# Transformer block with windowed attention and a spatially gated MLP: scores in 1024-column units with paired masks, overlapping contraction chunks, a new buffer plan and a new order

## The chip, the cores and the metric

The kernel runs on one core of one Trainium2 chip. The core has a matrix engine (TensorE, in the profile PE for multiplications and PEld for its weight loads), a vector engine (DVE), an activation engine (ACT), a general engine (POOL) and a queue that issues transfers (SP). TensorE writes to PSUM, eight banks of 512 float32 columns on 128 partitions; ACT and DVE read it from there. The metric is the device time of one execution, in microseconds (us), lower is better. The kernel before takes 363.6 us, the median of three runs (363.48 to 365.13).

## The reference

The input `x` has 2048 rows (tokens) of 448 columns, in bfloat16. A conditioning vector `c` gives six vectors of 448: shift and scale (`sa`, `ca`) and a gate `ga` for the first half, `sb`, `cb`, `gb` for the second.

```python
mod = (_silu(c) @ w_mod).reshape(c.shape[0], 6, 1, -1)
h = _layernorm(x) * (1 + ca) + sa
x = x + ga * _A_ref(h, A_wqkv, A_wo)          # 16 heads of 28; a row sees itself and the 255 rows before it
h = _layernorm(x) * (1 + cb) + sb
x = x + gb * _B_ref(h, ...)
# _B_ref: z = gelu(h @ w_in); z1 = z[:, :896]; z2 = layernorm(z[:, 896:])
#         g = w_sp @ z2 + b_sp;  result (z1 * g) @ w_out      (w_sp is 2048 x 2048)
```

## The kernel before, in words

The 2048 rows are 16 tiles of 128. All work is described as operations with dependencies, a priority and an assumed duration (class `Planner`, lines 55 to 211); when the kernel is built, a list scheduler places each operation on its engine at the earliest assumed start, ties and near ties by priority, and gives out PSUM banks and buffer slots as their last users end. The result is one fixed program for each engine, in which each instruction waits for semaphores. So an engine never goes past an instruction that waits, and the order on the chip is the order that the assumed durations led to. SP's queue is such a program too: a transfer's issue counts as 100 ns in the plan.

The work has four stages.

1. **Start.** Weights and `x` are loaded (lines 377 to 394), the conditioning vector is brought into columns by two transfers of single elements, `silu` is taken, and 32 one-column multiplications make shift and scale (`mod_cols`, 429). For each block of 512 rows (`NB` is 4) the rows are normalised (`ln1`, 498), transposed by TensorE (`transp`, 514), shifted and scaled on the way out of PSUM into `hT`, and multiplied by the weights (`qkv`, 548). The 448 rows of the contraction are cut into chunks of 128, 128, 128 and 64 (`KC`): four multiplications for each result. Q and K land in `QKT` with each head on its own 32 partitions, V in `Vaug` with a column of ones.
2. **Attention** (line 600 on), mixed with the projections of later blocks. For a tile j of queries and each of eight pairs of heads, one unit: up to 3 x 2 small multiplications (`S`, 611, on 32 rows of the array each) give the scores against key tiles j-2, j-1 and j; one ACT instruction takes the exponential of up to 768 columns (629); POOL zeroes what lies outside the window in tile j-2 and in tile j, with one instruction each (638, 640); six multiplications with 29 columns (`PV`, 652) add up the result and the sum of weights. After eight units, DVE divides (665, 667), SP issues a transposing transfer (671), four multiplications by `wo` follow (678), DVE adds to `x` (682), the second normalisation is taken (684 to 687), and a second transposing transfer writes `hT` anew (689). Scores have two pairs of banks (`B_S`), `PV` one bank, everything else three.
3. **MLP in** (line 742 on), after the last scores: `z2` for 16 tiles, `z1` for 28 blocks of 128 x 512, `gelu` on ACT, the normalisation of `z2` on DVE and POOL. Shift and scale of the second half were folded into `w_in` beforehand (702 to 714).
4. **Spatial product and MLP out** (line 782 on): 28 results of 16 multiplications each with the transposed `w_sp`, bias and product on DVE, 16 results of 7 multiplications by `w_out`, and the store. `w_sp` is loaded by 32 transposing transfers (728), which SP issues in the attention stage, two runs of 12 and one of 8.

## Time and profile before

One execution was profiled. Its span, from the first to the last instruction, is 362.0 us; the page gives no other time for that execution, and the runs' median is 1.6 us above the span.

| stretch of the span, us | what runs | length | TensorE busy | ACT busy | granted clock |
|---|---|---|---|---|---|
| 0 to 12.6 | loads, shift and scale | 12.6 | 2.45 | 1.58 | 1.00 |
| 12.6 to 62 | projections, first tiles | 49.4 | 46.76 | 27.65 | 0.97 |
| 62 to 92 | attention | 30.0 | 22.88 | 13.38 | 0.66 |
| 92 to 137 | attention and projections | 45.0 | 43.40 | 30.04 | 0.99 |
| 137 to 189.7 | attention alone | 52.7 | 42.90 | 36.46 | 0.50 |
| 189.7 to 240.1 | MLP in | 50.4 | 50.11 | 30.40 | 0.99 |
| 240.1 to 358.1 | spatial product, MLP out | 118.0 | 117.47 | 0.60 | 1.00 |
| 358.1 to 362 | last results and stores | 3.9 | 0.03 | 0.00 | 0.92 |

The granted clock is the share of full speed at which TensorE was allowed to run. A multiplication's duration contains its way through the array, so times are read here from one start to the next: where eight multiplications of 448 columns follow each other in the MLP stage the next group starts 1.52 us later, 0.190 us each. Where a line is L427, it is the helper `mm` through which all multiplications go; the tile names tell them apart.

### The profile page before, as it was taken

To read this page: it belongs to the slowest core of one execution; us is meant where nothing else is said; L and a number is where in the kernel's file an instruction comes from. 1 tells how busy PE (TensorE), PEld (TensorE's weight loads), DVE (VectorE), ACT (ScalarE), POOL (GpSimd) and SP (SyncE) were. 2 spreads that over 40 slices of the span, in tenths; PEclk is the share of its full clock that TensorE was granted. 3 is DMA by queue.
4 is the path that set the end of the run, shared out by engine and by line. 5 is a ranking of instruction groups with operands and counts; after the bars stand their busy time and mean duration, and the time that the engine had idled before them with its cause. 6 is when DMAs were issued, how large, how long until landed. Compare 5 with 4: busy or idle time off the path is not lost.

```text
span 362.0 us, 6545 instructions
## 1 busy us (share of the span) xinstructions
PE 326.0 (90%) x2620; PEld 156.6 (43%) x2648; DVE 171.7 (47%) x390; ACT 140.1 (39%) x197; POOL 117.4 (32%) x294
## 2 busy tenths in 40 slices
PE   0799998758999996698999999999999999999995
PEld 0424453423445553354444444444444444444442
DVE  1857645834576552232237887503324333233323
ACT  0346655633547675588784576640000000000000
POOL 5113344752648775588771212200000000000000
PEclk9999998955999995555559999999999999999999
DMA  6992399991212039813311000000001001001001
GB/s 200 344 347 82 59 177 168 185 173 29 45 31 30 16 40 167 118 31 46 30 31 29 16 0 2 2 0 0 2 0 51 2 0 53 0 0 39 14 0 51
DMA packets 60061, 23.62 MB, mean 65 GB/s; under 512 B 52224, under 2 KB 58560, under 8 KB 60032
## 3 DMA queue, kind: packets, MB, share of 16 engines
q1 hardware_dynamic: 59552, 23.21, 30.6%
q8 instruction: 21, 0.34, 0.4%
q10 hardware_dynamic: 480, 0.00, 0.1%
q14 instruction: 8, 0.07, 0.1%
HBM read 8.78 MB, written 1.84 MB: 29 GB/s over the span
## 4 chain that ended last, share of the span: by engine, by line
PE 80%; DMA 7%; SPq 4%; ACT 3%; DVE 3%; issue 2%; POOL 0%; DVEq 0%; ACTq 0%
PE ps L427 80%; DMA oT<-o_sb 5%; SPq L728 4%; ACT PT L629 3%; DMA cT_sb<-in_c_dram 2%; DVE w_out_sb L716 1%; DVE st_all L490 1%; DVE hT L534 0%; ACT L419 0%; DVE fin L820 0%; DVE WQK L542 0%; POOL rs_all L486 0%; DVE x_sb L682 0%; DVE sc_rep L421 0%; DVEq L829 0%
## 5 line engine op out<-in xcount | busy, mean ns | idle before, releaser
L629 ACT ACTIVATE PT<-ps 128x768 bf16<-128x768 f32 (+2 forms) x128 | 93.8, 770 | 55.3 <-PE ps L427 54.3
L427 PE MATMUL ps<-w_spA,z_73 128*128 128x512 bf16 x329 | 76.6, 379 | 0.4
L638 POOL TENSOR_SCALAR_AFFINE_SELECT PT<-PT 128x256 bf16<-128x256 bf16 x112 | 46.5, 415 | 52.9 <-ACT PT L629 51.9
L640 POOL TENSOR_SCALAR_AFFINE_SELECT PT<-PT 128x256 bf16<-128x256 bf16 x128 | 52.8, 414 | 21.3 <-ACT PT L629 21.2
L798 DVE TENSOR_TENSOR tmpg<-ps,bsp_bc 128x512 bf16<-128x512 f32 x28 | 19.4, 692 | 73.6 <-PE ps L427 73.6
L427 PE MATMUL ps<-QKT 32*128 32x128 bf16 x720 | 46.0, 257 | 6.2 <-ACT PT L629 4.8
L427 PEld LDWEIGHTS ps<-w_spA,z_73 128*128 128x128 bf16 x336 | 32.8, 98 | 39.6
L427 PE MATMUL ps<-hT,WQK 128*128 128x512 bf16 (+1 forms) x115 | 39.1, 412 | 1.5 <-ACT PT L629 0.4
L427 PE MATMUL ps<-Vaug,PT 128*128 128x29 bf16 x720 | 34.3, 183 | 2.3 <-POOL PT L640 1.9
L486 POOL TENSOR_TENSOR rs_all<-ve_all,neghalf 128x1 f32<-128x1 f32 (+1 forms) x39 | 23.0, 602 | 40.9 <-DVE ve_all L484 40.8
L427 PEld LDWEIGHTS ps<-Vaug,PT 128*128 128x128 bf16 x720 | 26.9, 101 | 20.4 <-POOL PT L640 7.6
L427 PE MATMUL ps<-wo_sb,oT 128*128 128x448 bf16 x64 | 23.2, 473 | 10.5 <-DMA oT<-o_sb 10.5
L427 PEld LDWEIGHTS ps<-QKT 32*128 32x128 bf16 x720 | 22.8, 105 | 22.0 <-PE ps L427 17.0
L682 DVE TENSOR_TENSOR x_sb<-ps,x_sb 128x448 bf16<-128x448 f32 x16 | 10.0, 624 | 40.3 <-PE ps L427 40.3
L427 PE MATMUL ps<-w_spB,z_73 128*128 128x512 bf16 x109 | 28.3, 379 | 0.2
L427 PE MATMUL ps<-w_in_sb,hT 128*128 128x448 bf16 (+1 forms) x128 | 26.8, 356 | 0.0
L427 PE MATMUL ps<-hT,w_in_sb 128*128 128x512 bf16 (+1 forms) x107 | 25.5, 379 | 0.3
L490 DVE BATCH_NORM_STATS2 st_all<-x_sb 128x6 f32<-128x448 bf16 x32 | 19.1, 611 | 6.6 <-DMA x_sb<-in_A_x_dram 6.3
L427 PE MATMUL ps<-w_out_sb,z1T 128*128 128x448 bf16 x112 | 21.8, 352 | 0.0
L567 DVE CAST QKT<-ps 128x512 bf16<-128x512 f32 x22 | 15.1, 688 | 13.3 <-PE ps L427 13.2
L490 DVE BATCH_NORM_STATS2 st_all<-z2raw 128x6 f32<-128x448 bf16 x32 | 18.7, 610 | 5.4 <-ACT z2raw L756 5.0
L776 ACT ACTIVATE z1T<-ps 128x512 bf16<-128x512 f32 x28 | 16.7, 597 | 8.6 <-PE ps L427 8.6
(65 smaller groups left out, 250.8 us busy)
## 6 DMA issues: line engine op xcount, KB each, us to landing
x_sb<-in_A_x_dram SPq DMA_DIRECT2D x4, 448.0 KB, 8.5
out_dram<-fin SPq DMA_DIRECT2D x16, 112.0 KB, 1.7
w_in_sb<-in_B_w_in_dram SPq DMA_DIRECT2D x1, 1344.0 KB, 11.4
wqkv_sb<-in_A_wqkv_dram SPq DMA_DIRECT2D x1, 1008.0 KB, 9.5
wmod_sb<-in_w_mod_dram SPq DMA_DIRECT2D x1, 1008.0 KB, 9.3
w_out_sb<-in_B_w_out_dram SPq DMA_DIRECT2D x1, 784.0 KB, 12.8
wmod_sb<-in_w_mod_dram SPq DMA_DIRECT2D x1, 672.0 KB, 7.3
bsp_bc<-in_B_b_sp_dram SPq DMA_DIRECT2D x1, 512.0 KB, 13.4
```

The costliest lines, as they stand in the source:

```text
L427: return e.matmul(out_, lhsT=lhsT, rhs=rhs, start=st, stop=sp, **kw)
L486: return P.op(name + "rs", prio, [("pool", 500 + 130 * (t1 - t0 - 1), lambda e: e.tensor_tensor(rs_all[:, slot, t0:t1], ve_all[:, slot, t0 ...
L490: st = [P.op("%sst%d" % (name, i), prio, [("dve", dve_ns(D, base=145), lambda e, i=i, s_=s_: e.bn_stats(st_all[:, slot, t, i, :], s_()))], ...
L567: return e.tensor_copy(QKT[:, g, tb * 512:(tb + 1) * 512], ps[:, ten.slot, :])
L629: return e.activation(ptv(pt)[:, :, 0:nb, :], ps[:, ten.slot:ten.slot + 2, 0:nb * 128].rearrange("p h (b q) -> p h b q", q=128), ACT.Exp, ...
L638: e.affine_select(out=v[:, :, 0, :], in_=v[:, :, 0, :], pattern=[[0, 2], [-1, 128]], compare_op=ALU.is_gt, fill=0.0, base=0, channel_multi ...
L640: return e.affine_select(out=v[:, :, nb - 1, :], in_=v[:, :, nb - 1, :], pattern=[[0, 2], [1, 128]], compare_op=ALU.is_ge, fill=0.0, base= ...
L682: x1_op[j] = P.op("x1_%d" % j, pr, [("dve", 624, lambda e, j=j, wt=wt: e.tensor_tensor(x_sb[:, j, :], ps[:, wt.slot, 0:D], x_sb[:, j, :], ...
L716: t_woutg = P.op("woutg", 4.3, [("dve", dve_ns(7 * D), lambda e: e.tensor_tensor(w_out_sb[:], w_out_sb[:], ps[:, ten_g2.slot, 0:D].unsquee ...
L728: return e.dma_start_transpose(out=dst[:, hf * 1024:(hf + 1) * 1024], in_=B_w_sp[hf * 1024:(hf + 1) * 1024, si * 128:(si + 1) * 128])
L776: z1_op[(ft, tb)] = P.op("z1g%d_%d" % (tb, ft), pr, [("act", act_ns(512), lambda e, tb=tb, ft=ft, ten=ten: e.activation(z1T[:, ft, tb * 51 ...
L798: a = P.op("ga%d_%d" % (tb, ft), pr, [("dve", 692, lambda e, tb=tb, ten=ten, tg=tg: e.tensor_tensor(tmpg[:, tg.slot, :], ps[:, ten.slot, : ...
```

## The change

Nearly every function is written anew. In the order of the stages:

- **Start.** The conditioning vector is loaded as one row and turned into columns by four small multiplications; the tables of `silu` and of the exponential are loaded ahead of their first use; 30 multiplications of zeros (`warm`) may fill TensorE's idle time. Loads that only the second half needs (`w_in`, the second part of `w_mod`, `w_out`, the bias) are issued after the first four transposing transfers. The blocks are 256, 256, 512, 512 and 512 rows. From the third block on, rows are normalised on POOL, transposed by a transfer on SP, and shifted and scaled in place by DVE or POOL (`modulate`).
- **Chunks.** The 448 rows of a contraction are held as four chunks of 128 that overlap (rows 0, 128, 192 and 320 on), so that two results (`Pair`) take three whole multiplications each, and their rests, 64 rows in the upper and 64 in the lower half of the array, one double step. The order takes the rests of two pairs together. Q, K, V, `z2` and `z1` are made so. Other contractions use four chunks of 112.
- **Attention.** A unit is one key tile with eight heads: 8 multiplications into two banks, one exponential of 1024 columns that reads the two banks element by element in turn, so that the results of two heads lie side by side. For key tiles j and j-2 POOL masks 512 such pairs as 32-bit words with one instruction; for j-1 none. The eight `PV` multiplications read their stationary operand with a step of two elements. There are 90 units in place of 128, 60 masks in place of 240.
- **Rest.** Shift and scale of the second half are no longer folded into `w_in` but applied to `hT`, two tiles at a time; `PV`, `wo` and the projections share banks 4 to 7. `w_sp` is fetched in 32 transfers of 512 x 256: 16 go into parts of `QKT` as their last scores are done (4 each after tiles 5, 9, 13 and 15), 16 into `Vaug` and `PT` after the last `PV`. Assumed durations and priorities are new (SP's transposing issue now counts 1250 to 1340 ns). Stage 4 has the same multiplications.

```diff
+WINDOW = {'pe': 60.0, 'act': 0, 'dve': 200.0, 'pool': 0, 'sp': 100}
+PARAMS = {
+    'ln1': (-43.888, -27.425, 1.986, 3.811, 5.635),
+    'tr': (-50.231, -2.58, 0.847, 3.1, 3.297),
+    'pj': (-38, -0.204, 1.282, 3.815, 6.655),
+    'st': (0.017, 0.046, 0.3, 0.5, 0.266),
+    'gateA': 2.025,
+    'modB': 2.249,
+    'gateB': 10.911,
+    'pv': -42.625,
+    'wo': 1.33,
+    'x1': -3.81,
+    'l2': 5.98,
+    'rest': -100.0,
+    'hold': 0,
+    'batch': ((15, (0, 1, 2, 3, 4, 5, 6, 7, 8, 9, 10, 11, 12, 13, 14, 15), (0, 1, 2, 3)),),
...
+    FULL_A, FULL_B = (0, 3, 1), (0, 3, 2)
+    BLOCKS = ((0, 2), (2, 2), (4, 4), (8, 4), (12, 4))
+    blk = [i for i, (t0, n) in enumerate(BLOCKS) for _ in range(n)]
...
+    B_S = banks((0, 1), (2, 3))
+    B_ONE = banks((4,), (5,), (6,), (7,))
+    B_TWO = banks((4, 5), (6, 7), (5, 6))
+    B_Z = B_TWO + B_S
+    B_Z1 = B_ONE + banks((0,), (1,), (2,), (3,))
+    B_LOW = banks((0,), (1,), (2,), (3,))
...
+    def load_w(name, prio, dst, w, a, b, order=(), eng="sp", o=0):
         n = b - a
-        l1 = load(name + "a", prio, lambda e: e.dma_start(dst[:, 0:3, o:o + n], big), 384 * n * 2)
-        l2 = load(name + "b", prio + 0.001, lambda e: e.dma_start(dst[0:64, 3, o:o + n], small), 64 * n * 2)
-        return [l1, l2]
...
+    t_c = load("c", -100, lambda e: e.dma_start(crow[0:1, :], c), 896, eng="act")
+    t_x = [None] * 5
+    t_x[0] = load_x("x0", -99, 0, 2)
+    t_wmA = load_112("wmodA", -98, wmod_sb, w_mod, 0, 2 * D)
+    t_wqk = load_w("wqk", -95.5, wqk_raw, A_wqkv, 0, 904)
+    t_x[1] = load_x("x1", -96, 2, 2)
+    t_wv = load_w("wv", -97, wv_sb, A_wqkv, 2 * D, 3 * D, o=2 * D)
+    t_x[2] = load_x("x2", -94, 4, 4)
+    t_wmG = load_112("wmodG", -93, wmod_sb, w_mod, 2 * D, 3 * D)
+    t_wo = load_112("wo", -92, wo_sb, A_wo, 0, D)
+    t_x[3] = load_x("x3", -91, 8, 4)
+    t_x[4] = load_x("x4", -90, 12, 4)
...
+    t_silu0 = P.op("silu0", -61, [("act", 180, lambda e: e.activation(one[:, 8:9], one[:, 0:1], ACT.Silu))], [t_one], table="silu")
...
+    t_cc = pe("c_cols", -60, 400, c_fn, [t_c, t_one], [tc_ten], mode=32)
+    t_sc = P.op("silu", -59, [("act", 180, lambda e: e.activation(sc_sb[0:112, :], ps[0:112, tc_ten.slot, 0:4], ACT.Silu))],
+                [t_cc, t_silu0], [tc_ten], table="silu")
+    t_exp0 = P.op("exp0", -58, [("act", 180, lambda e: e.activation(one[:, 9:10], one[:, 0:1], ACT.Exp))], [t_sc], table="exp")
...
+    def modulate(name, prio, c_, cols, n, base_col, deps):
+        def f(e):
+            return e.tensor_scalar(hT[:, c_, cols], hT[:, c_, cols], modT[:, base_col + 4 + c_:base_col + 5 + c_],
+                                   modT[:, base_col + c_:base_col + c_ + 1], ALU.mult, ALU.add)
+        return P.op(name, prio, [("dve", dve4_ns(n), f), ("pool", pool_ns(n), f)], deps, port=True)
...
+    def transp_dma(b, pr):
+        t0, n = BLOCKS[b]
+        trs = []
+        for t in range(t0, t0 + n):
+            trs.append(P.op("hx%d" % t, pr, [("sp", 1250, lambda e, t=t: e.dma_start_transpose(
+                out=hT[:, :, t * 128:(t + 1) * 128], in_=xn[:, xn_ten[t].slot, :]))], [xn_op[t]], [xn_ten[t]], table="tr", dma=(131072, 190.0, 1000)))
+        hT_op[b] = [modulate("hT%d_%d" % (b, c_), pr + 0.1, c_, slice(t0 * 128, (t0 + n) * 128), 128 * n, 0, trs + t_modA) for c_ in range(4)]
+        return trs
...
+            self.ops = []
+            for i, (full, stat, mov, deps) in enumerate(((FULL_A, stat_a, mov_a, deps_a), (FULL_B, stat_b, mov_b, deps_b))):
+                ten = joint if joint else self.tens[i]
+                for c_ in full:
+                    o = [None]
+
+                    def fn(e, i=i, c_=c_, stat=stat, mov=mov, o=o):
+                        a = acc[i]
+                        return mm(e, out_ap(i), stat(c_, slice(0, 128)), mov(c_, slice(0, 128)), a.first is o[0], a.last is o[0])
+                    o[0] = pe("%s_%s%d" % (name, "ab"[i], c_), prio, mm_ns(n), fn,
+                              [deps] + ([kdeps[c_]] if kdeps else []), [ten], order=order if not self.ops else self.ops[:1], accs=[acc[i]], pair=self.tens)
+                    self.ops.append(o[0])
+            r = [None]
+
+            def rest(e):
+                mm(e, out_ap(0), stat_a(2, slice(64, 128)), mov_a(2, slice(64, 128)), acc[0].first is r[0], acc[0].last is r[0], tile_position=(64, 0))
+                return mm(e, out_ap(1), stat_b(1, slice(0, 64)), mov_b(1, slice(0, 64)), acc[1].first is r[0], acc[1].last is r[0], tile_position=(0, 0))
+            r[0] = pe(name + "_r", prio if rprio is None else rprio, mm_ns(n) + 10, rest, [deps_a, deps_b] + ([kdeps[1], kdeps[2]] if kdeps else []), self.tens,
+                      order=self.ops[:1], mode=64, accs=acc, hold=hold, pair=self.tens)
+            self.ops.append(r[0])
+
+
...
+    t_win = load_w("win", -10, w_in_sb, B_w_in, 0, 2 * FH, order=trs[:4])
+    t_wmB = load_112("wmodB", -9, wmod_sb, w_mod, 3 * D, 6 * D, order=trs[:4])
+    t_wout = load("wout", 2.5, lambda e: e.dma_start(w_out_sb[:], B_w_out.rearrange("(f p) n -> p f n", p=128)), FH * D * 2, order=trs[:4])
+    t_bsp = load("bsp", 2.6, lambda e: e.dma_start(bsp_bc[:], B_b_sp[:].partition_broadcast(128)), 128 * S * 2, order=trs[:4])
...
+        units = [(kb, gp) for kb in (j - 2, j, j - 1) if kb >= 0 for gp in (0, 1)]
...
+            def s_fn(e, j=j, kb=kb, gp=gp, ten=ten):
+                for n_ in range(8):
+                    g, s_ = n_ // 2, n_ % 2
+                    hh = 2 * gp + s_
+                    last = mm(e, ps[:, ten.slot + s_, g * 128:(g + 1) * 128], QKT[32 * hh:32 * hh + DH, 4 + g, kb * 128:(kb + 1) * 128],
+                              QKT[32 * hh:32 * hh + DH, g, j * 128:(j + 1) * 128], True, True, tile_position=(32 * hh, 0))
...
+            s_op = pe("S%d_%d" % (j, ui), pr - 50, 135, s_fn, deps, [ten], mode=32, order=all_S[-1:])
...
+            e_op = P.op("E%d_%d" % (j, ui), pr, [("act", act_ns(1024), lambda e, ten=ten, pt=pt: e.activation(
+                PT[:, pt.slot, :, :], ps[:, ten.slot:ten.slot + 2, :].rearrange("p b n -> p n b"), ACT.Exp, scale=SCALE))],
...
+            if kb != j - 1:
+                pat, cm, cmp = ([[0, 4], [1, 128]], -1, ALU.is_ge) if kb == j else ([[0, 4], [-1, 128]], 1, ALU.is_gt)
+                ready = pool("M%d_%d" % (j, ui), pr - 50, pool_ns(512), lambda e, pt=pt, pat=pat, cm=cm, cmp=cmp: e.affine_select(
+                    out=pt32(pt.slot), in_=pt32(pt.slot), pattern=pat, compare_op=cmp, fill=0.0, base=0,
+                    channel_multiplier=cm), [e_op], [pt])
...
+                for n_ in range(8):
+                    g, s_ = n_ // 2, n_ % 2
+                    h = 4 * g + 2 * gp + s_
+                    last = mm(e, ps[:, pv_ten.slot, 32 * h:32 * h + DH + 1], PT[:, pt.slot, g * 128:(g + 1) * 128, s_],
+                              Vaug[:, kb, h, 0:DH + 1], acc.first is o[0] and n_ == 0, acc.last is o[0] and n_ == 7, skip_group_check=True)
...
+            o[0] = pe("PV%d_%d" % (j, ui), pr + G["pv"], 8 * 26, pv_fn, [ready, V_op[kb]], [pt, pv_ten], accs=[pv_acc])
...
+            wos.append(pe("wo%d_%d" % (j, kc), pr + G["wo"], mm_ns(D), lambda e, oTt=oTt, wt=wt, kc=kc: mm(
+                e, ps[:, wt.slot, 0:D], oT[0:112, oTt.slot, kc, :], wo_sb[0:112, kc, :], kc == 0, kc == 3), [t1, t_wog], [oTt, wt], order=wos[-1:]))
...
+            pair = Pair("z2m%d" % t, pr + 0.01 * (zi // 2), None, [h2_op[t], t_win], [h2_op[t], t_win], hst, lambda c_, r: w_in_sb[r, c_, FH:FH + D],
+                        hst, lambda c_, r: w_in_sb[r, c_, FH + D:FH + 2 * D], D, order=[S_op[(T, nu - 2)]], joint=joint,
+                        rprio=pr + 0.01 * (zi // 2) + 0.005, hold=0)
...
+            for f0 in (0, 2, 4):
+                zp = pr + 0.05 + 0.01 * (f0 // 4)
+                pair = Pair("z1m%d_%d" % (tb, f0), zp, opts, h2d, h2d, wst1(f0), hmv, wst1(f0 + 1), hmv, 512,
+                            order=[S_op[(T, nu - 2)]], rprio=zp + 0.005, hold=0)
...
+    for tb in range(4):
+        for p_ in range(8):
+            def fn(e, tb=tb, p_=p_):
+                src = B_w_sp[tb * 512:(tb + 1) * 512, p_ * 256:(p_ + 1) * 256]
+                si = 2 * p_
+                if tb < 2:
+                    dst = QKT[:, si % 8:si % 8 + 2, tb * 1024 + (si // 8) * 512:tb * 1024 + (si // 8) * 512 + 512]
+                else:
+                    dst = (w_spC if tb == 2 else w_spD)[:, si:si + 2, :]
+                return e.dma_start_transpose(out=dst, in_=src)
+            if tb < 2:
+                lastt = (5 if p_ < 4 else 9) if tb == 0 else (13 if p_ < 4 else 15)
+                deps = [S_op[(lastt, 2 * min(lastt + 1, 3) - 1)]]
+            else:
+                deps = all_PV
...
+            early = tb == 0 and ft < 4
+            ten = Ten(B_LOW if early else B_ALL)
...
+    w_ten = Ten(banks((3,)))
+    warm_ops = []
+    for i in range(30):
+        warm_ops.append(pe("warm%d" % i, 1000, 216, lambda e: mm(e, ps[:, w_ten.slot, :], warm[:, 0:128], warm[:], True, True), [t_warm], [w_ten],
+                           order=warm_ops[-1:]))
```

## The prediction

> **What bounds the kernel now.** I read the page for the span, then busy time by stretch of the span, then TensorE's instructions in order of time. The stretches say which stages have air in them:
>
> ```profile
> core 0: us, PE busy (x) PEld busy (x) DVE busy (x) ACT busy (x) POOL busy (x), PEclk, DMA share, GB/s
> 62.00:92.00 30.00, 22.88 (x254) 10.44 (x258) 17.01 (x37) 13.38 (x18) 16.21 (x39) 0.66 0.68 121
> 92.00:137.00 45.00, 43.40 (x581) 22.80 (x588) 27.39 (x55) 30.04 (x39) 31.23 (x82) 0.99 0.26 37
> 137.00:189.70 52.70, 42.90 (x587) 22.91 (x584) 16.90 (x43) 36.46 (x48) 37.95 (x102) 0.50 0.45 69
> 189.70:240.10 50.40, 50.11 (x258) 24.00 (x260) 33.97 (x92) 30.40 (x44) 10.08 (x18) 0.99 0.04 9
> 240.10:358.10 118.00, 117.47 (x551) 54.59 (x559) 38.75 (x69) 0.60 (x1) 0.00 (x0) 1.00 0.04 12
> ```
>
> From 189.7 on TensorE is full at full clock: 168 us that only fewer multiplications can shorten. The air is before it: 62 to 92 with 7 us idle and the clock at 0.66, and 137 to 189.7 at half clock. From 92 to 137 the stage runs as well as it can, and gives the prices. By starts (start, length, ..., count):
>
> ```profile
> 100.43 0.34 PE L427 MATMUL ps<-QKT 32*128 32x128 bf16 x6
> 100.70 1.14 PE L427 MATMUL ps<-hT,WQK 128*128 128x512 bf16 x4
> 101.78 0.34 PE L427 MATMUL ps<-QKT 32*128 32x128 bf16 x6
> 102.05 1.03 PE L427 MATMUL ps<-wqkv_sb,hT 128*128 128x448 bf16 x4
> 103.01 0.39 PE L427 MATMUL ps<-hT,WQK 128*128 128x512 bf16 x1
> ...
> 107.93 0.36 PE L427 MATMUL ps<-QKT 32*128 32x128 bf16 x12
> 108.22 0.32 PE L427 MATMUL ps<-Vaug,PT 128*128 128x29 bf16 x6
> ...
> 110.23 0.30 PE L427 MATMUL ps<-Vaug,PT 128*128 128x29 bf16 x6
> 110.47 0.34 PE L427 MATMUL ps<-QKT 32*128 32x128 bf16 x6
> ```
>
> A score unit of six takes 0.27, and two in a row only 0.29: different rows of the array work at once, and most of the price is the change of mode. It also lengthens the `PV` ahead of it (0.24 before scores; 0.15 at 99.65 before a projection, so 0.026 for each of six). Hence 0.355 for a lone unit. A Q or K group takes 1.08 and a V group 0.96, where four whole multiplications take 0.87 and 0.76 in the MLP stage: the last chunk of 64 rows costs 0.2 more.
>
> The stretch at half clock:
>
> ```profile
> 178.54 0.50 PE L427 MATMUL ps<-QKT 32*128 32x128 bf16 x6
> 178.99 0.34 PE L427 MATMUL ps<-Vaug,PT 128*128 128x29 bf16 x6
> 179.33 0.50 PE L427 MATMUL ps<-QKT 32*128 32x128 bf16 x6
> 179.76 1.78 PE L427 MATMUL ps<-wo_sb,oT 128*128 128x448 bf16 x4
> 181.48 0.50 PE L427 MATMUL ps<-Vaug,PT 128*128 128x29 bf16 x12
> ```
>
> Scores 0.44, `PV` 0.27 to 0.34, `wo` 1.72: a tile takes 7.9 us (171.9 to 179.8). What the middle waits for, by SP's queue and TensorE's wait:
>
> ```profile
> 41.18 17.81 SPq L728 DMA_TRANSPOSE w_spA<-in_B_w_sp_dram  x12
> 61.71 17.69 SPq L728 DMA_TRANSPOSE w_spA<-in_B_w_sp_dram  x12
> 82.19 1.76 PE L427 MATMUL ps<-wo_sb,oT 128*128 128x448 bf16 x4 [4.31 <-DMA oT<-o_sb]
> ```
>
> Twice SP issues 12 transfers of `w_sp` in nearly 18 us, and the transposes of `oT` stand behind them.
>
> **The change, part by part.** All sums are against the span of 362.0; the runs' median is 1.6 above it.
>
> *Contractions in the attention stage.* Q and K: before, 32 groups at 1.08, 34.6. After, 16 pairs of 512 columns' worth, seven steps of 0.216: 24.2. V: 16 x 0.96 = 15.4 becomes 8 x 7 x 0.190 = 10.6. This takes two 64-row multiplications as running at once; the scores' 0.29 for two units speaks for it. Each visit to the rests changes mode (0.2, from the 64-row groups): 28 pairs, rests by twos, 14 x 0.2 = 2.8; bounds 0 and 28 x 0.2 = 5.6. If the two halves ran one after the other, 4.5 more. `wo` loses its 64-row chunk: 16 x 0.97 = 15.5 becomes 16 x 0.76 = 12.2.
>
> *Scores and `PV`.* Eight multiplications use two row groups, four times 128 columns in each; a quarter of 0.216 is 0.054, so a lone unit is 0.27 + 0.054 + 0.085 = 0.41, 90 of them 36.5; as adjacent twos (0.29 + 0.054 + 0.085) 19.3. I take 33, since few units were adjacent before. Before: 128 units, 43. `PV`: 720 x 0.026 = 18.7 in both. Its stationary operand now has a step of two elements, which no row shows: bounds 0.026 and twice that, plus 18.7. I take no change, as the weight load of the same shape (101 ns) already overlaps.
>
> *Small items.* The 64 transposes by TensorE at 0.075 become 16 (4.8 to 1.2); 16 bias multiplications of 0.2 go (4.0); shift, scale and gates stay at about 6.4.
>
> TensorE's attention work: before 34.6 + 15.4 + 43 + 18.7 + 15.5 + 15 = 142; after 24.2 + 10.6 + 2.8 + 33 + 18.7 + 12.2 + 8 = 109. The old sum ran from 12.6 to 189.7, 177 us: 35 were lost to the cold start, SP and half clock.
>
> *ACT.* Eight exponentials of 768 columns at 182.45 take 6.09 us, 0.754 apart; two of 512 at 40.24 are 0.53 apart; so 1024 columns are 0.97, and 90 make 87 us (before 128: 92). The reading of two banks by turns is in no row: bounds 0.97 and 1.82 (twice per column); I take 0.97, since ACT's write in runs of 28 (line 584, 543 ns for 448, where 597 for 512 in one piece would give the same) costs nothing extra. With half the evictions of Q, K and V, 14 us, ACT needs 101: close behind TensorE.
>
> The Trainium skill speaks against this read: "PSUM — Partial Sum Buffer", Specifications (TRN2), gives PSUM 8-byte lines and says that a non-contiguous pattern slows matmuls significantly. If that held for ACT's read at one line for each column, the sum would be the 365.6 of rival C in place of 306.6; no row here shows it.
>
> *POOL, DVE, SP.* Masks: 240 x 0.36 = 86 become 60 x 0.61 = 37 (128 columns 292 ns, 256 columns 415, so 512 add 0.25; if a 32-bit word costs double, 68). Twelve normalisations of 0.6 move to POOL; 44 in-place shifts of some 0.35 come to DVE or POOL (15), and 12 evictions of 0.8, the folding into `w_in` and its casts go (18). DVE is busy 27 of 45 in the dense stretch, so I cost these at nothing; uncovered, they would add 15. SP gets 12 more transposes at 1.26, 76 issues in all, 97 us over a stage of 125. An `oT` now stands behind one `w_sp` issue, not twelve: both blocks go, and the four `wo` after them. Behind a late `oT` stand `x1`, the second normalisation and `hT` for the MLP stage, which uses the tiles in turn and needs the last one 20 us later. The last 20 issues, 26 us, lie beside MLP and spatial product.
>
> *Start.* `c` lands at 8.3 us today and holds the first multiplication to 10.15; as one row it should land by 3, and then `w_mod` (0.8 MB behind 0.23 MB, at the 344 GB/s of the page's second slice, plus some 3 us) is the wait, 6 to 7. Table loads leave the chain. I take TensorE's start of real work at 11 in place of 12.6, first scores at 16 in place of 22.8.
>
> *Clock.* With scores first and projections as filling, TensorE stays full until the last block is projected, before tile 12: 109 less the last four tiles (24 units at 0.41, `PV` 5, `wo` 3: 18) is 91, at 92% (96% before, but `PV`, pairs and `wo` now share four banks) 99. The last four have no filling; at the rates of the half-clock lines a unit is 0.44 + 0.107 for the fourth 128 columns, and its `PV` 0.28 + 2 x 0.026, so 24 x 0.88 + 4 x 1.72 = 28. Bounds: 23, if ACT's 24 x 0.97 decides at full clock, and 46, if half clock begins four tiles earlier (10 for the units, 8 for a block's projection). The added wait is the pair's: it needs two of banks 4 to 7 empty, and in TensorE's fixed order the scores behind it wait too, and ACT behind those; that is the 4% between 96 and 92. The MLP stage begins at 11 + 99 + 28 = 138, less 3 for the last exponentials, which it covers: 135.
>
> "TensorE: Matmul & The Clock Gate", Part 1, has the clock drop after an idle window of about 3.4 us. Here it stays at 0.50 from 137 to 189.7 with no gap above 2.6 us; by the page the last tiles would take 23, and the sum would be 5 lower.
>
> *MLP in.* 112 x 0.190 + 100 x 0.216 = 42.9, 16 mode changes of 0.2 (3.2), the last `wo` and `PV` 2: 48.1 against 50.4. ACT's 28 and DVE's 34 lie inside. The first pairs now wait for the in-place shift of `hT`; nothing but MLP work stands behind them, and tiles 0 to 13 are shifted while the last scores run. *Spatial and out:* unchanged, 118.0, and 3.9.
>
> Sum: 135 + 48.1 + 118.0 + 3.9 = 305.0, with 1.6 for what lies around: 306.6; I say 306.
>
> **Rivals.**
> A. *ACT decides, at full clock.* For it: ACT needs 101, TensorE 109, and doubled units occur. First exponential at 16, then 101: MLP at 117, total 117 + 48.1 + 118 + 3.9 + 1.6 = 288.6.
> B. *The filling fails*: `PV` weights at double (+19), half clock from tile 8 on (+18), or banks 4 to 7 holding TensorE at 80% (+15). For it: four banks carry what four carried before, but a pair needs two at once. One of these gives 321 to 325, two about 342.
> C. *Slower: the interleaved read costs double.* 90 x 1.82 = 164 plus 14 of evictions from 16 on: MLP at 194, total 365.6; from 1.80 us for each exponential on it is slower than 363.6. Against it: no row shows a stride that costs ACT time.
> D. *The change does little*, because half clock holds for the whole stage: Q, K and V twice 35 (70), 90 x 0.88 = 79, `wo` 27, the rest 11, from 11 on: MLP at 198, total 369.6. Against it: 92 to 137 held 0.99 with the same mix.
>
> **How the numbers follow.** My own case (295 to 318) 0.50, A 0.18, B 0.20, C 0.06, D 0.03, others 0.03. The range leaves out half of C, D and the far ends: 287 to 342. A measurement can tell some 0.5% here, 1.8 us. Faster 0.89, same 0.03, slower 0.08.
>
> **What would show it.** The exponential's line at 128x1024: about 1.05 us long (C: 1.9). MLP's first multiplication at about 135 (A 117, D 198). No `oT` wait above 2 us. Granted clock above 0.9 up to some 110 us, then about half. Masks at 0.65 us. Rests starting together. Spatial stage still 118. Wrong it would be through an in-order wait on banks 4 to 7, or a clock that drops early.

## The result and the profile after

The changed kernel takes 308.34 us (median of four runs, 305.90 to 310.85); in the same comparison the kernel before took 364.05. The ratio is 0.845, with a 95% interval of 0.840 to 0.851. The prediction said 306, in a range of 287 to 342.

The profiled execution, the fastest of the four, has a span of 304.1 us, where the prediction's sum gave 305.0. That near hit hides two misses of 8 to 9 us with opposite signs, as the busy time by stretch of the span shows (core 0; stretch, its length, then busy time and count for PE, PEld, DVE, ACT and POOL; at the end the granted clock, the DMA share and GB/s):

```profile
13.80:38.60 24.80, 24.10 (x359) 14.21 (x357) 22.09 (x57) 22.45 (x36) 17.25 (x25) 1.00 0.59 164
38.60:47.80 9.20, 7.16 (x109) 3.64 (x104) 3.64 (x10) 4.32 (x7) 3.13 (x5) 1.00 1.28 272
47.80:68.30 20.50, 20.49 (x220) 9.28 (x220) 7.92 (x17) 13.51 (x14) 10.78 (x17) 0.51 0.56 107
68.30:112.30 44.00, 44.00 (x727) 24.92 (x728) 22.07 (x49) 41.11 (x46) 18.45 (x30) 1.00 0.35 62
112.30:131.10 18.80, 18.80 (x337) 10.81 (x335) 16.51 (x37) 18.43 (x19) 8.91 (x15) 1.00 0.69 102
131.10:197.00 65.90, 63.36 (x339) 26.19 (x340) 38.90 (x111) 31.01 (x47) 19.23 (x34) 1.00 0.56 102
197.00:300.10 103.10, 103.10 (x493) 47.85 (x490) 40.16 (x74) 0.00 (x0) 0.54 (x1) 1.00 0.04 14
```

The attention stage ends at 131 in place of 189.7, and this is the whole gain: from there to the end it is 173 us, before 172. Two rows are not as predicted. From 47.8 to 68.3 the clock is at half, early in the stage, where the prediction had it full. From 112.3 to 131.1, the last four tiles, it is full, where the prediction had it at half. ACT is busy 41.1 of 44.0 and 18.4 of 18.8: from 68 on it is as full as TensorE.

In the last tiles a score unit, now eight multiplications, stands like this in TensorE's order of time (start, length, line and operation):

```profile
122.56 0.40 PE L444 MATMUL ps<-QKT 28*128 28x128 bf16 x8
122.89 0.36 PE L444 MATMUL ps<-Vaug,PT 128*128 128x29 bf16 x8
123.10 0.54 PE L444 MATMUL ps<-wo_sb,oT 112*128 112x448 bf16 x2
123.57 0.40 PE L444 MATMUL ps<-QKT 28*128 28x128 bf16 x8
```

From start to start, the scores take 0.33 and eight `PV` multiplications 0.21, 0.026 each, as before. A unit comes every 1.01. The half-clock stretch begins here:

```profile
40.87 3.30 PE L444 MATMUL ps<-hT,WQK 128*128 128x512 bf16 x15
45.73 0.54 PE L444 MATMUL ps<-sc_sb,wmod_sb 112*128 112x1 bf16 x16 [1.56 <-DMA wmod_sb<-in_w_mod_dram]
46.20 0.42 PE L444 MATMUL ps<-QKT 28*128 28x128 bf16 x16
46.56 0.55 PE L444 MATMUL ps<-sc_sb,wmod_sb 112*128 112x1 bf16 x16
46.97 0.35 PE L444 MATMUL ps<-wv_sb,hT 128*128 128x448 bf16 x1
47.81 0.40 PE L444 MATMUL ps<-QKT 28*128 28x128 bf16 x8 [0.49 <-ACT PT L768]
...
49.33 0.60 PE L444 MATMUL ps<-QKT 28*128 28x128 bf16 x8
49.87 1.30 PE L444 MATMUL ps<-wv_sb,hT 128*128 128x448 bf16 x3
51.10 0.60 PE L444 MATMUL ps<-QKT 28*128 28x128 bf16 x8
```

Fifteen projections follow one another with no scores between. Then TensorE waits 1.56 us for the second part of `w_mod`, the largest wait of the stage, and does 32 multiplications of one column; after that a unit takes 1.7 us. There are twelve such units up to 68.3. At the later rate of 1.03 they would have taken 8 us less.

SP's queue at that point, with the time that its issues take:

```profile
31.63 1.09 SPq L453 DMA_DIRECT2D w_in_sb<-in_B_w_in_dram  x2
32.76 0.47 SPq L457 DMA_DIRECT2D wmod_sb<-in_w_mod_dram  x1
...
34.13 4.38 SPq L730 DMA_DIRECT2D bsp_bc<-in_B_b_sp_dram  x1
38.55 6.95 SPq L620 DMA_TRANSPOSE hT<-xn  x2
```

The second part of `w_mod` lands 12.8 us after its issue, behind `w_in`. The two blocks of twelve `w_sp` transposes are gone, and TensorE has no wait for an `oT` left in the attention stage; in the kernel before there were five, 10.5 us together. The groups by form (busy us, mean ns) carry the prediction's prices:

```profile
L768 ACT ACTIVATE PT<-ps 128x1024 bf16<-128x1024 f32 x90 | 90.1, 1030 | 12.6 <-PE ps L444 11.8
L775 POOL TENSOR_SCALAR_AFFINE_SELECT PT<-PT 128x512 f32<-128x512 f32 x60 | 38.0, 636 | 47.7 <-ACT PT L768 47.5
```

Executions of one kernel differ by several us, with granted clocks that differ too (0.938 to 0.966 in these four), so the ratios leave out those more than 1.5% above the fastest, and small differences of time are judged by the traces.

### The profile page after: what moved, and what is told of

It is laid out like the page before. It is cut to its first block, busy times and chain, and to the rows that moved or that the text cites. A ratio compares the mean times of both kernels' runs of the same rounds, so it can differ in the third digit from the quotient of the medians.

```text
span 304.1 us, 6216 instructions
## 1 busy us (share of the span) xinstructions
PE 293.6 (97%) x2650; PEld 142.6 (47%) x2650; DVE 159.4 (52%) x377; ACT 136.1 (45%) x173; POOL 82.5 (27%) x135
## 4 chain that ended last, share of the span: by engine, by line
PE 83%; DMA 6%; DVE 5%; POOL 3%; ACT 1%; SPq 1%; issue 1%; DVEq 0%; POOLq 0%; ACTq 0%
PE ps L444 83%; DMA wmod_sb<-in_w_mod_dram 4%; DMA hT<-xn 2%; DVE st_all L534 2%; POOL hT L612 1%; DVE wo_sb L734 1%; DVE o_sb L798 1%; ACT z2raw L845 1%; POOL PT L775 1%; POOL rs_all L542 1%; DVE mv_all L537 0%; DVE z L556 0%; DVE fin L950 0%; SPq L453 0%; ACT PT L768 0%
## 5 line engine op out<-in xcount | busy, mean ns | idle before, releaser
L768 ACT ACTIVATE PT<-ps 128x1024 bf16<-128x1024 f32 x90 | 90.1, 1030 | 12.6 <-PE ps L444 11.8
L775 POOL TENSOR_SCALAR_AFFINE_SELECT PT<-PT 128x512 f32<-128x512 f32 x60 | 38.0, 636 | 47.7 <-ACT PT L768 47.5
L444 PE MATMUL ps<-QKT,z 128*128 128x512 bf16 x224 | 49.5, 379 | 0.0
L444 PE MATMUL ps<-QKT 28*128 28x128 bf16 x720 | 37.3, 228 | 0.7 <-ACT PT L768 0.7
L444 PE MATMUL ps<-hT,WQK 128*128 128x512 bf16 (+3 forms) x160 | 37.5, 358 | 0.0
L444 PEld LDWEIGHTS ps<-QKT,z 128*128 128x128 bf16 x224 | 21.5, 98 | 26.8 <-issue 1.6
L444 PEld LDWEIGHTS ps<-QKT 28*128 28x128 bf16 x720 | 21.2, 97 | 25.3 <-issue 15.6
L542 POOL TENSOR_TENSOR rs_all<-ve_all,neghalf 128x1 f32<-128x1 f32 (+2 forms) x29 | 18.7, 647 | 49.6 <-DVE ve_all L541 49.4
L444 PE MATMUL ps<-w_spC,z 128*128 128x512 bf16 x112 | 24.5, 379 | 0.0
L444 PE MATMUL ps<-w_spD,z 128*128 128x512 bf16 x112 | 24.5, 379 | 0.0
L845 ACT ACTIVATE z2raw<-ps 128x896 bf16<-128x896 f32 x16 | 14.5, 916 | 19.2 <-PE ps L444 12.8
L444 PE MATMUL ps<-wv_sb,hT 128*128 128x448 bf16 (+1 forms) x64 | 18.5, 403 | 0.0
## 6 DMA issues: line engine op xcount, KB each, us to landing
wmod_sb<-in_w_mod_dram SPq DMA_DIRECT2D x1, 1176.0 KB, 12.8
```

Of the source, the lines that this page charges most:

```text
L444: return e.matmul(out_, lhsT=lhsT, rhs=rhs, start=st, stop=sp, **kw)
L542: r = pool(name + "rs", prio, 420 + 148 * n, lambda e: e.tensor_tensor(rs_all[:, slot, t0:t1], ve_all[:, slot, t0:t1], neghalf[:, t0:t1], ...
L768: e_op = P.op("E%d_%d" % (j, ui), pr, [("act", act_ns(1024), lambda e, ten=ten, pt=pt: e.activation(PT[:, pt.slot, :, :], ps[:, ten.slot:t ...
L775: ready = pool("M%d_%d" % (j, ui), pr - 50, pool_ns(512), lambda e, pt=pt, pat=pat, cm=cm, cmp=cmp: e.affine_select(out=pt32(pt.slot), in_ ...
L845: g = P.op("z2g%d" % t, pr - 20, [("act", act_ns(FH), lambda e, joint=joint, zt=zt: e.activation(z2raw[:, zt.slot, :].rearrange("p (a d) - ...
```

## The experiments

My theory after the result: the early half-clock stretch costs 8 us and is caused by what stands at 41 to 48; in the last tiles the clock holds, and ACT and TensorE are level. The rivals: ACT alone decides; the interleaved read, the pairing of masks or the rests carry more than I priced; SP's cost in the plan alone explains the gain.

**The load put first.** `w_mod`'s second part is issued ahead of `w_in`.

```diff
-    t_wmB = load_112("wmodB", -9, wmod_sb, w_mod, 3 * D, 6 * D, order=trs[:4])
+    t_wmB = load_112("wmodB", -11, wmod_sb, w_mod, 3 * D, 6 * D, order=trs[:4])
```

> The edit: the load of the second part of w_mod is issued ahead of the two loads of w_in; every other queue keeps its order. In the changed kernel TensorE waits 1.56 us for it at 44.2, gives ACT no scores from 38.3 to 46.2, and from 47.8 to 68.3 its granted clock is 0.51: 12 score units take 20.5 us, 1.71 each, where later ones take 1.03. Theory 1 (the wait starts the half clock): the wait goes, the clock stays at 1.00, 12 units at 1.03 save 8 us and the wait 1.5, so the MLP stage's first multiplication comes at 120 to 122 in place of 130, and the time is 298 to 300 against 308.3. Theory 2 (the clock falls through the light work beside it, 32 one-column groups and the scores without projections, or for a reason of the chip's own): the wait goes and the clock falls all the same, first MLP multiplication at 128 to 129, time 306.5 to 307.5. Theory 3 (the wait only moves, because w_in's 1.6 MB are then late for something): 308 or above, with a new DMA wait of TensorE in the list.

Measured: 306.86 (302.41 to 312.34). The wait for `w_mod` is gone, but the clock was at half twice, for 10.2 and 20.5 us. The first time, from 33.3 on, it follows another wait, where the changed kernel's first profile has one of 0.54:

```profile
30.13 0.40 PE L444 MATMUL ps<-QKT 28*128 28x128 bf16 x8
31.65 0.54 PE L444 MATMUL ps<-wo_sb,oT 112*128 112x448 bf16 x2 [1.13 <-DMA oT<-o_sb]
```

The second is where it was, behind the same one-column multiplications, with no wait above 0.5. So the wait for `w_mod` is not the cause by itself; Theory 2 stands. The first stretch need not be this edit's doing: a second profile of the changed kernel without an edit, reported below, has half clock from 33.6 too, after a wait of 0.68, and no wait for `w_mod` either. Two of the four executions took 302.41 and 304.11, so a gain of a few us is not excluded.

**The burst moved away.** `w_in`, `w_out` and the bias are issued behind all twelve transposes of the input.

```diff
-    t_win = load_w("win", -10, w_in_sb, B_w_in, 0, 2 * FH, order=trs[:4])
+    t_win = load_w("win", -10, w_in_sb, B_w_in, 0, 2 * FH, order=trs)
...
-... FH * D * 2, order=trs[:4])
+... FH * D * 2, order=trs)
...
-... 128 * S * 2, order=trs[:4])
+... 128 * S * 2, order=trs)
```

> The edit: the loads of w_in (two), w_out and of the spatial bias, spread to all partitions, are ordered behind the twelve transposes of the input's normalised rows in place of the first four; the planner orders the queues anew. In the changed kernel SP sits 4.38 us in the issue of the bias load and 6.95 in the next two transposes while these loads move 240 to 380 GB/s, TensorE then waits for w_mod's second part, and with that load put first it waits for an oT instead: in both cases the granted clock halves between 34 and 48. Theory 1 (the burst of loads makes the gaps, and the gaps make the half clock): the transposes take 1.3 each, no wait of TensorE above 1 us between 28 and 60, clock 1.00 up to the MLP stage; MLP's first multiplication at 120 to 123, time 297 to 301. Theory 2 (the fixed order of TensorE makes the hole: fifteen projections with no scores between, for which ACT starves): ACT still gets no scores for 5 us or more near 40 to 46, the clock may fall behind it, gain 0 to 4: 304 to 308. Theory 3 (the burst then meets the transposes of oT later): the half clock moves to 60 to 80, time 306 to 310.

Measured: 308.24 (305.64 to 311.75), so no gain. The transposes still took 4.57 for three and 3.54 for two, so the short transposes of Theory 1 did not come about, and the half clock began in the same place, at 47.6, and lasted 37.5 us:

```profile
40.66 3.30 PE L444 MATMUL ps<-hT,WQK 128*128 128x512 bf16 x14
43.89 0.55 PE L444 MATMUL ps<-sc_sb,wmod_sb 112*128 112x1 bf16 x16
44.65 0.43 PE L444 MATMUL ps<-QKT 28*128 28x128 bf16 x16 [0.21 <-ACT QKT L691]
45.01 0.55 PE L444 MATMUL ps<-sc_sb,wmod_sb 112*128 112x1 bf16 x16
46.26 0.40 PE L444 MATMUL ps<-QKT 28*128 28x128 bf16 x8 [0.48 <-DVE xn L555]
```

Between 32 and 47 no wait is above 0.5, so no single one is left that could be blamed; what is left is a stretch with little in it.

**The one-column work moved.** To the later loads, the second modulation gets its place by tile 5. In this run, as in the one above, the planner orders all queues anew, so other work moves too.

```diff
-    'modB': 2.249,
+    'modB': 5.0,
```

> The edit: beside the later loads of w_in, w_out and the bias, the 32 one-column groups of the second modulation get their place by tile 5 in place of 2.249, so they leave the stretch at 44 to 47, where TensorE has the fifteen projections behind it, ACT has nothing to do and the clock has fallen in every run so far. Five whole V multiplications now follow the fifteen directly. Theory 1 (the small work together with the gaps of 1 to 2.5 us lowers the clock): no gap above 0.5 between 40 and 50, clock 1.00 up to the MLP stage, 12 units at 1.03 in place of 1.71, so 8 us less than the changed kernel beside it: 298 to 301 where that has 308. Theory 2 (ACT's hole alone is enough: the scores behind it run one per exponential and leave TensorE part idle): half clock from about 46 all the same, less than 3 us gained.

Measured: 302.71 (297.21 to 320.81), at a ratio to the kernel before of 0.816 (0.804 to 0.827). The changed kernel without an edit, in the same runs, took 307.80 (305.25 to 311.94), at 0.837 (0.831 to 0.844). The half clock at 48 is gone. In the fastest execution the mean granted clock was 1.00: 297.21. In the profiled one it falls at 66.6, 1.5 us after the last of the one-column groups, and again nothing waits for long there:

```profile
63.40 0.40 PE L444 MATMUL ps<-QKT 28*128 28x128 bf16 x8
63.73 0.35 PE L444 MATMUL ps<-sc_sb,wmod_sb 112*128 112x1 bf16 x8
64.17 0.40 PE L444 MATMUL ps<-QKT 28*128 28x128 bf16 x8
...
67.48 0.60 PE L444 MATMUL ps<-QKT 28*128 28x128 bf16 x8
```

Theory 1 as I wrote it, small work together with gaps, is half right: the 8 us at 48 go with the one-column work, but here the clock falls behind that work without gaps. That the small work causes this fall is argued from its place alone. By the medians this version beats both kernels, the changed one by 5 us, but one of its six executions, at 320.81, was slower than all of the changed kernel's.

> The changed kernel once more, without an edit, as the measure for the three runs beside it on one chip. If the chip sets the time of a kernel as it did of the one before (363.6 to 369 in different jobs), it comes out at 308 to 313, at a ratio of 0.845 to the one before. The half-clock stretch behind the wait for w_mod begins at 46 to 48 in every profile so far, and ended at 68 to 84 in kernels that keep the changed kernel's order there.

Measured: 307.80 at 0.837, so the changed kernel's own time moved little from one comparison to the other, though the kernel before took 368.93 beside it, where it had taken 364.05. Its profile had two half-clock stretches, from 33.6 (10.2 us) and from 50.7 (27.3 us), so the 46 to 48 that I expected in every profile was wrong too.

**Evictions off ACT.** In the same version, DVE alone evicts Q, K and V of blocks 3 and 4.

```diff
-... [("act", act_ns(w), ev_a), ("dve", dve_ns(w), ev_d)], pair.ops, [ten])
+... ([("act", act_ns(w), ev_a)] if b < 3 else []) + [("dve", dve_ns(w), ev_d)], pair.ops, [ten])
```

The evictions of V are changed in the same way, and the planner orders the queues anew.

> The edit: as the run before it in this list, and the Q, K and V evictions of blocks 3 and 4 are left to DVE alone; in the changed kernel ACT does about eight of them, 0.54 to 0.59 each, 4.6 us. Theory 1 (ACT decides from 68 to 131, where it is busy 41.1 of 44 and 18.4 of 18.8): 4 to 5 us less than the run before it, with ACT's exponentials 1.00 apart from about 50 on and the first MLP multiplication that much earlier. Theory 2 (TensorE decides, whose busy time is all of that stretch by the profile): less than 1 us. Theory 3 (DVE, at 0.69 each, gives the banks back later, and the pairs that need two of four banks hold TensorE up): slower than the run before it, with waits of TensorE on DVE.

Measured: 306.31 (297.46 to 308.53). No gain is seen. The cleanest pair are the two executions that held the clock at 1.00 throughout: 297.46 here, 297.21 without the edit. ACT's whole-size evictions in the attention stage fell from 7.4 to 4.1 us by the two profiles, 3.3 in place of the 4.6 that I had reckoned, and brought nothing. That speaks against Theory 1, ACT alone. Theory 3's waits on DVE are not there: one, of 0.5 us, in the whole stage. A single pair cannot tell a gain of 0.5 us, and with the orders changed it is no clean proof.

**A stall in ACT, late and early.** Three exponentials whose result is not used, ahead of one unit of tile 13 or of tile 9.

```diff
+... [e.activation(z2raw[...1024 columns, i_...], ps[:, ten.slot:ten.slot + 2, :]..., ACT.Exp, scale=SCALE) for i_ in range(3)]
 ... e.activation(PT[:, pt.slot, :, :], ps[:, ten.slot:ten.slot + 2, :]..., ACT.Exp, scale=SCALE)
```

> The edit: ahead of the exponential of tile 13's first unit, ACT runs the same exponential three more times into a buffer that is idle then; the result is not used and every queue keeps its order. ACT is held up by 3 x 1.00 us, and so is TensorE's next score unit. After this point no Q, K or V projection is left. Theory 1 (half clock follows a gap of TensorE, and only a run of large multiplications ends it): the clock falls to about 0.5 from there to the MLP stage; the 18 units left take some 0.44 + 0.107 for the scores, 0.28 + 0.05 for PV and their share of wo, 0.88 + 0.29 = 1.17 each in place of 1.02, so 3.1 + 2.7 = 6 us more: 314. Theory 2 (a gap alone does not lower the clock, ACT simply decides here): 3.1 more, 311.4, the clock at 1.00. Theory 3 (TensorE decides in this stretch and ACT has slack): less than 2 more.

> The same edit at tile 9's first unit, at some 88 us, with projections of the last block still to come. Theory 1: the gap lowers the clock, and the next dense run of projections raises it again, so 3.1 plus at most 5 us (the half-clock stretch of the changed kernel cost 8 us over 12 units): 311.5 to 316, with a stretch at half clock that ends before the last projections do. Theory 2: 3.1 more, 311.4, clock at 1.00 throughout. If TensorE and not ACT decides between 68 and 112, less than 2 more: below 310.3.

Measured: late 316.87 (316.27 to 317.70), 8.5 more than the changed kernel; early 313.76 (312.82 to 315.48), 5.4 more. TensorE late, then early:

```profile
118.30 0.61 PE L444 MATMUL ps<-QKT 28*128 28x128 bf16 x8 [2.17 <-ACT PT L769]
118.84 1.30 PE L444 MATMUL ps<-wo_sb,oT 112*128 112x448 bf16 x3
```

```profile
93.25 0.61 PE L444 MATMUL ps<-QKT 28*128 28x128 bf16 x8 [2.16 <-ACT PT L769]
...
97.92 1.15 PE L444 MATMUL ps<-hT,WQK 64*128 64x512 bf16 x3
99.00 0.40 PE L444 MATMUL ps<-QKT 28*128 28x128 bf16 x8
```

The same gap of 2.2 us halves the clock in both. Late, it stays at half for 27.3 us, through the last tiles and into the MLP stage; early, where projections follow, for 6.8. Theory 1 holds, and the late cost is 2 to 3 us larger than I reckoned from the lines of before.

**Plain reads.** Each exponential reads its banks one after the other, and `PV`'s stationary operand has a step of one.

```diff
-PT[:, pt.slot, :, :], ps[:, ten.slot:ten.slot + 2, :].rearrange("p b n -> p n b"), ACT.Exp
+PT[:, pt.slot, :, :].rearrange("p n s -> p (n s)").rearrange("p (b n) -> p b n", b=2), ps[:, ten.slot:ten.slot + 2, :], ACT.Exp
...
-PT[:, pt.slot, g * 128:(g + 1) * 128, s_]
+PT[:, pt.slot, :, :].rearrange("p n s -> p (n s)")[:, s_ * 512 + g * 128:s_ * 512 + (g + 1) * 128]
```

> The edit: each exponential reads its two banks one after the other in place of by turns, writes its 1024 columns in that order, and PV's stationary operand has a step of one element in place of two. Every queue keeps its order. What it changes of the computation: the mask still clears 32-bit pairs, which are now neighbours in one head, so the masked scores are not the reference's. If reading two banks by turns and the step of two cost nothing (the prediction took this), the exponential stays at 1030 ns and about 1.00 apart, eight PV multiplications at 0.21 from start to start, and the time at 308 within 1. If the read by turns costs something that 1030 ns hides, it falls towards 0.97 apart: 90 x 0.03 = 2.7, time near 305. If the step of two costs TensorE, PV becomes shorter than 0.21 and the half-clock stretch, where TensorE decides, shortens by 1 or 2 us.

Measured: 308.57 (306.49 to 312.54).

```profile
L768 ACT ACTIVATE PT<-ps 128x1024 bf16<-128x1024 f32 x90 | 90.3, 1029 | 18.7 <-PE ps L444 18.0
L444 PE MATMUL ps<-Vaug,PT 128*128 128x29 bf16 x720 | 30.9, 179 | 0.9 <-issue 0.8
```

1029 ns against 1030, and `PV` is no shorter: 179 ns against 178 by the groups, and 0.21 for eight from start to start in both. Neither the read by turns nor the step of two costs anything that these rows show.

**Rests one after the other.** Both halves of a rest use the same 64 rows.

```diff
-mm(e, out_ap(1), stat_b(1, slice(0, 64)), mov_b(1, slice(0, 64)), ..., tile_position=(0, 0))
+mm(e, out_ap(1), stat_b(1, slice(64, 128)), mov_b(1, slice(64, 128)), ..., tile_position=(64, 0))
```

> The edit: the second half of every rest is put on the same 64 rows of the array as the first. What it changes of the computation: that half multiplies 64 rows of its chunk that are counted already, in place of the 64 that are missing, so the contraction is not the reference's. Every queue keeps its order. Theory 1 (the two halves run at once in the changed kernel, as the prediction took): each pair gets some 0.2 us longer; in the MLP stage, where TensorE decides, 16 x 0.19 + 12 x 0.216 = 5.6 us more (169 becomes 175 from the first MLP multiplication to the end); in the attention stage 28 x 0.2 = 5.6 of work, of which ACT hides between all and none: 314 to 320. Theory 2 (they run one after the other already): nothing changes, 308.

Measured: 344.52 (314.06 to 360.99): the clock was at half for 78.5 us in the profiled execution, so the time says little; that the longer rests are why it did not come back was not tested. The fastest execution, 314.06 at a mean clock of 0.960, is the one to set beside the changed kernel's 305 to 309 at 0.960 to 0.966: 5 to 9 us more, within Theory 1. The groups speak more clearly. First the changed kernel's rests of the MLP stage, then this one's:

```profile
L444 PE MATMUL ps<-hT,w_in_sb 64*128 64x512 bf16 x28 | 4.8, 380 | 0.0
L444 PE MATMUL ps<-w_in_sb,hT 64*128 64x448 bf16 x32 | 4.8, 356 | 0.0
```

```profile
L444 PE MATMUL ps<-w_in_sb,hT 64*128 64x448 bf16 x32 | 7.8, 352 | 0.0
L444 PE MATMUL ps<-hT,w_in_sb 64*128 64x512 bf16 x28 | 7.4, 379 | 0.0
```

2.6 and 3.0 more, 5.6 in all, as Theory 1 had it: the two halves do run at once in the changed kernel.

**Masks not paired.** Two masks of 16-bit words for each unit.

```diff
-e.affine_select(out=pt32(pt.slot), in_=pt32(pt.slot), pattern=pat, ...)
+[e.affine_select(out=PT[:, pt.slot, :, s_]..., in_=PT[:, pt.slot, :, s_]..., pattern=pat, ...) for s_ in range(2)][-1]
```

> The edit: each mask over 512 words of 32 bits becomes two over 512 words of 16 bits, every other word each, with the same output; every queue keeps its order. POOL's masks are 38.0 us in the changed kernel, and POOL is busy 58 us of the 117 between 14 and 131. If a mask costs by the word, as 636 ns for 512 words of 32 bits says beside 0.61 worked out from 16-bit masks, the masks become 76 and POOL is busy 96 of 117. Theory 1 (masks are hidden, since PV stands well behind the exponential): time within 1.5 of 308. Theory 2 (POOL's normalisations of blocks 2 to 4 and the masks share the first 40 us, where POOL is busy 17 of 25): the projections of block 2 come later, TensorE waits in front of them, 311 to 318. A mask of 16-bit words at half the price, 0.32, would leave POOL and the time as they are and tell that pairing saved only the instruction's fixed part.

Measured: 326.80 (324.74 to 329.96), 18.5 more, beyond Theory 2's 318, and the wait is another than Theory 2 had: for the masks themselves. POOL's group, then TensorE's largest wait:

```profile
L775 POOL TENSOR_SCALAR_AFFINE_SELECT PT<-PT 128x512 bf16<-128x512 bf16 x120 | 85.3, 771 | 22.7 <-ACT PT L768 22.6
```

```profile
PE ps L444 <- POOL PT L775: 8.1, 15, 1.1
```

Fifteen waits for masks, 8.1 us together, and the clock at half for 51.2 us in place of 20.5. With 85 us of masks POOL is on the path. In the kernel before it hardly was: its profile has 99 us of masks (128 at 414 ns and 112 at 415), yet TensorE waited for them four times, 2.0 us together, between 12 and 200.

**SP's cost corrected, in the kernel before.** Only the planner's cost of a transpose's issue is corrected; the planner then orders all queues anew, TensorE's too.

```diff
-        t1 = P.op("oT%d" % j, pr, [("sp", 100, lambda e, ...
+        t1 = P.op("oT%d" % j, pr, [("sp", 1250, lambda e, ...
```

The transposes into `hT` get 1250 too, and those of `w_sp` 1480.

> The kernel before, with only the planner's cost of a transpose's issue on SP corrected from 100 ns to what its trace shows (1250 for a tile, 1480 for w_sp), so that it no longer puts twelve w_sp transposes in a row ahead of an oT. It tells how much of the 55 us lies in SP's order alone. The prediction: the lost time of the old stage is 35 us of cold start, SP and half clock, with 4.31 us of wait for oT and 7 us of idle TensorE at a clock of 0.66 between 62 and 92. Theory 1 (SP's two blocks cost what the stretch shows): 7 us of idle and some 5 of half clock go, 349 to 353 against 363.6. Theory 2 (the loss only moves, since the half clock of 137 to 189.7 stays and may begin earlier): within 3 of the time before. Theory 3: w_sp then comes later than the spatial product needs it: slower than before, with a wait of the spatial stage.

Measured: 351.80 (349.43 to 352.85), at a ratio of 0.957 (0.948 to 0.967) to the kernel before beside it: about 4%, some 15 us. By stretch, for comparison with the prediction's rows:

```profile
62.00:92.00 30.00, 28.20 (x357) 13.66 (x361) 21.08 (x43) 19.54 (x26) 21.52 (x53) 0.89 0.68 117
...
137.00:175.00 38.00, 34.67 (x463) 18.94 (x463) 13.42 (x35) 29.36 (x39) 31.16 (x84) 0.50 0.32 60
```

From 62 to 92, 5.3 us of idle time are gone and the clock is 0.89 in place of 0.66, and of the five waits for an `oT` none is left. The half-clock tail stays. Theory 1 holds: the corrected cost, with the orders that follow from it, is worth somewhat more than a quarter of the gain. How much of that is SP's order and how much TensorE's was not tested.

**Without the warming multiplications.** The 30 at the start get 16 columns.

```diff
-mm(e, ps[:, w_ten.slot, :], warm[:, 0:128], warm[:], True, True)
+mm(e, ps[:, w_ten.slot, 0:16], warm[:, 0:128], warm[:, 0:16], True, True)
```

> The edit: the 30 multiplications at the start whose result is not used are cut from 512 columns to 16; every queue keeps its order. In the kernel before, which has none, the clock is at half until some 22 us: three multiplications of 512 columns take 1.71 at 16.57, where 0.65 is the price at full clock. Theory 1 (they hold the clock up while TensorE waits for data): the block from 9.04 to 19.02 then runs at half clock; its real work is 32 multiplications of 256 columns (3.4 at full clock), 8 of 448 (1.5), the transposes and the gate (2.5), 7 us, less the 2 of the warming among it: first scores at 21 to 24 in place of 19, and the time 3 to 5 longer. Theory 2 (that stretch waits for loads and evictions): first scores at 19 within 0.5, time within 1.

Measured: 307.75 (306.60 to 311.11). First the changed kernel, then this one:

```profile
9.04 0.64 PE L444 MATMUL ps<-sc_sb,wmod_sb 112*128 112x1 bf16 x20
...
11.59 1.64 PE L444 MATMUL ps<-wv_sb,hT 128*128 128x448 bf16 x8
```

```profile
7.37 0.69 PE L444 MATMUL ps<-sc_sb,wmod_sb 112*128 112x1 bf16 x20 [4.35 <-DMA wmod_sb<-in_w_mod_dram]
...
10.54 2.92 PE L444 MATMUL ps<-wv_sb,hT 128*128 128x448 bf16 x8 [1.14 <-DVE hT L605]
...
19.32 0.42 PE L444 MATMUL ps<-QKT 28*128 28x128 bf16 x16
```

Eight V multiplications take 2.92 in place of 1.64, so TensorE is indeed slow there, and the scores still start at 19.32 in place of 19.02: Theory 2's number. But waits are not the whole reason. In the changed kernel twelve warming multiplications take 3.42 us from 5.78 on, ahead of the first use of `w_mod`, which comes 1.7 us later for it, and the first projection 1.05 later. What the warming gives in speed, it had cost just before.

## Why the prediction came out right

**Contractions.** Right: seven steps for a pair, the halves of the rests at once, and the change of mode at 0.2 for each visit. One pair of the MLP stage, six whole multiplications and one rest, and what follows it:

```profile
191.18 1.59 PE L444 MATMUL ps<-w_in_sb,hT 128*128 128x448 bf16 x8
192.71 1.90 PE L444 MATMUL ps<-QKT,z 128*128 128x512 bf16 x8
```

From start to start it takes 1.53, where seven steps of 0.189 are 1.32: 0.20 are left for the visit. The stage shows 17 visits; the thirteen that stand between whole multiplications, with no wait and no record missing, cost 0.20 each, however many rests stand together. So the 3.2 us charged there were needed, and the 2.4 us of waits for `z2raw` and `hT` came on top.

**Scores and `PV`.** Right: 0.33 for the scores, some 0.08 on a `PV` ahead of them, 0.026 for each `PV`. The bound "plus 18.7" for the strided stationary operand is out.

**ACT.** Right: thirteen exponentials in 13.03 us, 1.00 apart, where I took 0.97. Rival C's doubled read did not happen. The Trainium skill, "PSUM — Partial Sum Buffer", Specifications (TRN2), warns that non-contiguous patterns slow matmuls; the row for ACT's read shows no such cost, 1030 ns against 1029.

**POOL, DVE, SP.** The new masks came out right (38.0 where I had 37), by luck in part: the 0.36 for an old one is in no row of theirs, which read 0.41, 99 us in place of 86, and a new one worked out from that would be 0.66. The normalisations on POOL took 0.79 (I had 0.6), and the 44 shifts 21.7 us (I had 15). That I costed all this at nothing was right, since between 14 and 131 TensorE waited for POOL never and for DVE once, 0.5 us; but the cover on POOL was thin, as the 18.5 us for unpaired masks show. For SP I had both blocks going, and they went. Its price was short: single transposes beside loads took up to 3.6 us, where I had 1.26.

**Start.** `w_mod` lands at 7.5 (I had 6 to 7), its first use comes at 9.04, behind the warming, and the first projection at 11.59 (I had 11). The scores come at 19.02, not 16: the planner puts the 32 Q and K multiplications of the first block, the eight transposes of the second and the gate ahead of them. Mis-sized by 3.

**Clock.** This step failed. "The last four have no filling; at the rates of the half-clock lines", 28 us: they took 18.8 at full clock, and the 18 of work that I had priced for them filled it. And "TensorE stays full until the last block is projected" failed at 47.8, where 8 us went. What I missed, as far as the windows below show it: not the filling as such goes with the clock, but how much work a short window holds, and the last tiles hold enough. A stall of 3 us there would have made my half-clock tail true, as the late stall shows.

**Sum.** From the first projection to the last four tiles it took 100.7 us (11.59 to 112.3) where I had 99: the 8 us of half clock stand in the place of the 8 that I had allowed for shared banks. From there to the first MLP multiplication it took 17.7 in place of 28 less 3. So the MLP stage began at 130.0 where I had 135, and from there to the end it took 174.1 where I had 170.0, 2.4 of it waits: 304.1 against 305.0. That the sum came within 1 us is luck: 5 us too long up to the MLP stage and 4.1 too short behind it, with the half clock in the wrong place.

**Rivals.** A described the stretch from 68 on better than my own case did, since ACT is full there; but TensorE is too. At full clock throughout, with the one-column work moved, the time is 297, between A's 288.6 and my 306. B's early half clock came, for another reason and for 20 us only.

## What to carry to other kernels

A price list from a dense stretch carries far: TensorE's and ACT's prices held within 0.05 us. The misses were in the clock, in the start, and in POOL's, DVE's and SP's prices, which did not change the time. When you forecast a tail of small multiplications, do not ask only whether filling is left but, by the reading below, how much of the array's time a window of 3.4 us uses, in rows and columns; and put a light group of instructions, or a short wait, where large multiplications follow (6.8 us of half clock there, 27.3 in the tail). When two engines are level, as ACT and TensorE here, taking work from one brought nothing that was seen, and a stall of ACT cost all of its length and some of the clock too.
